# Attention and mixture of experts on one core: a constant tile 96 bytes longer, six staging tiles for weights instead of four, and an offset for one block of the first expert

## The chip, the cores and the metric

The kernel runs on one core of one Trainium2 chip. The metric is the time of one execution on the device in microseconds (us); the median of several runs counts. The engines are named as in the profile: PE (matrix products), PEld (PE's loading of weights), DVE (VectorE), ACT (ScalarE), POOL (GpSimd) and SP (SyncE, which here issues transfers).

## What is computed

The reference has two halves. The first is attention for 2 batches of 8 heads, 768 tokens and 64 columns a head, where a token looks only at the tokens with its own hash bucket. The second sends each of the 1,536 rows of 512 columns that come out to one of 8 experts:

```python
h = np.maximum(x[b, s] @ w1[e], 0.0)
out[b, s] = p[e] * (h @ w2[e])
```

Here `w1[e]` is 512 x 1024 and `w2[e]` is 1024 x 512, in float32. Routing is top 1, and a row may keep the expert of the row before it.

## The kernel before

The attention half comes first. An order written out by hand (`ORDER`) sets what each engine does there. It ends at about 251 us with the rows of the first expert gathered and transposed. From then on the experts follow one another, 256 slots each, and a scheduler of the language orders the instructions on each engine.

An expert has two layers. **The hidden layer** (`hidden`, L688) has four blocks of 24 matmuls with 256 moving columns each. Every float32 operand is split into a high and a low part (`wh` and `wl`, `xH` and `xL`, `hH` and `hL`), and three of the four products are summed. The weights of `w1` are the stationary operand (`lhsT`), the rows of x the moving one. After each block ACT writes `hH` (L690) and DVE writes `hL` (L691). **The output layer** (`expert`, L798) has for each half of the slots (t = 0 and 1) 24 matmuls with 512 moving columns. Here `hH` and `hL` are stationary and the parts of `w2` move. The last expert cuts its second half into two pieces of 256 columns. Between the two layers of an expert, eight transposes (`xprep`, L765) turn the rows of the next expert. Expert 0 differs: its weights and rows come through tiles left from the attention half.

**Weights** (`weights`, L750) come in pieces of 512 KB, four of `w1` and four of `w2` an expert. SP issues the transfer into a staging tile `st` of the pool `wst` (L752), ACT makes `wh` (L754), DVE makes `wl` (L755). The staging tile is free again after L755. The parts of `w1` have room for one expert (`w1p`, 8 tiles), those of `w2` for two (`w2p`, 16 tiles). The rows of expert e+1 (`xsl`, L761) come through the same queue of SP into one of two tiles. That tile is free when the scatter of expert e-1 to the output has landed (`out`, L808, issued by POOL).

**Addresses.** Pools are laid out from both ends of a partition's memory. From the left, in this order, stand among others the constants with `OV` in their middle, `w2p`, `hp` (`hH`, `hL`) and `mp` (`xsl`, `xH`, `xL`). From the right stand `wst`, then `w1p`. The tiles are placed by the program, not by chance, and the addresses that follow are those of the built program. `XOFF` (40 words) shifts `xH` and `xL` inside their tiles, and `HOFF` shifts the last of the four blocks of `hH` and `hL` of the experts that it names, by words of 4 bytes:

```python
HOFF = {1: 62, 2: 62, 3: 32, 4: 16, 5: 62, 6: 16}
hH, hL = (wide(hp, [128, 2, 256], n, HOFF.get(e, 0) if i == 3 else 0, 64) for n in ("hH", "hL"))
xH, xL = (wide(mp, [128, 4, 256], n, XOFF, 64) for n in ("xH", "xL"))
```

By distance this text means the address at which the running matmul begins to read its moving operand, less the address from which the next matmul's weights are loaded, modulo 256 bytes.

Of the kernel before, what the change touches and what calls it, by code (L numbers as in the profile page):

```python
# [6 lines left out]
F32 = mybir.dt.float32  # L7
# [9 lines left out]
CAP = 256  # L17
NE = 8
XOFF = 40
HOFF = {1: 62, 2: 62, 3: 32, 4: 16, 5: 62, 6: 16}  # L20

# [95 lines left out]
def tile_kernel(ctx, tc, qT, kT, v, proj, wg, w1, w2, cst, out):  # L119
    nc = tc.nc  # L120
    const = ctx.enter_context(tc.tile_pool(name="const", bufs=1))
# [30 lines left out]

    xs = dram.tile([NE * CAP, 514], F32, name="xs")
    xo = dram.tile([5 * CAP, 514], F32, name="xo")
    OV = const.tile([1, 16], F32, name="OV")
    ni = const.tile([1, 1], I32, name="ni")
    be = const.tile([1, 5], I32, name="be")
    EC = [const.tile([128, 2, 6, 8], F32, name=f"ec{b}") for b in range(2)]
# [242 lines left out]
    def fill_some(k):  # L401
        for _ in range(min(k, len(fills))):
            o, i = fills.pop()
            nc.sync.dma_start(out=o, in_=i)

    def fill(dst, z, zi):
        n = dst.shape[0] // 128
        nc.gpsimd.memset(z, 0.0)
        nc.gpsimd.iota(zi, pattern=[[128, n]], base=2048, channel_multiplier=1)
        xv = dst.rearrange("(t p) c -> p t c", p=128)  # L410
        fills.extend((xv[:, o:o + m, 0:513], z[:, 0:513].unsqueeze(1).to_broadcast([128, m, 513])) for o in range(0, n, 2) for m in (2,))
        with nc.allow_non_contiguous_dma(reason="one word per row"):
            nc.sync.dma_start(out=xv[:, :, 513].bitcast(I32), in_=zi)
# [103 lines left out]
    def overflow_count():  # L517
        row = [const.tile([1, 8], F32, name=f"cr{i}") for i in range(2)]
        nb = const.tile([1, 8, 5], F32, name="nb")
        nc.sync.dma_start(out=row[0], in_=CU[1])  # L520
        nc.vector.tensor_tensor(out=row[1], in0=row[0], in1=cs[0:1, 144:152], op=ALU.subtract)
        nc.vector.scalar_tensor_tensor(out=nb, in0=row[1].unsqueeze(2).to_broadcast([1, 8, 5]), scalar=1.0 / CAP,
                                       in1=cs[0:1, 188:193].unsqueeze(1).to_broadcast([1, 8, 5]), op0=ALU.mult, op1=ALU.is_gt)
        nc.vector.tensor_reduce(out=row[1], in_=nb, axis=AX.X, op=ALU.add)
        nc.vector.tensor_tensor_scan(out=OV[:, 8:16], data0=row[1], data1=row[1], initial=0.0, op0=ALU.add, op1=ALU.max)
        nc.vector.tensor_tensor(out=OV[:, 0:8], in0=OV[:, 8:16], in1=row[1], op=ALU.subtract)
        nc.vector.tensor_copy(out=ni, in_=OV[:, 15:16])
        bt = const.tile([1, 5, 8], F32, name="bt5")
        bf = const.tile([1, 5], F32, name="bf5")
        nc.vector.tensor_tensor(out=bt, in0=OV[:, 8:16].unsqueeze(1).to_broadcast([1, 5, 8]),  # L530
                                in1=cs[0:1, 188:193].unsqueeze(2).to_broadcast([1, 5, 8]), op=ALU.is_le)
        nc.vector.tensor_reduce(out=bf, in_=bt, axis=AX.X, op=ALU.add)
        nc.vector.tensor_copy(out=be, in_=bf)
# [136 lines left out]
    def wide(pool, shape, name, o, pad):  # L670
        n = shape[1] * shape[2]
        return pool.tile([128, n + pad], F32R, tag=name, name=name)[:, o:o + n].rearrange("p (a b) -> p a b", a=shape[1])

    def hidden(e, W1, X1, between=None):
        hs = []
        for i in range(4):
# [9 lines left out]
            for k, n in order:  # L686
                w, x = terms[k][n]
                nc.tensor.matmul(out=hps[:, k], lhsT=w, rhs=x, start=(k, n) in ends[0], stop=(k, n) in ends[1])  # L688
            hH, hL = (wide(hp, [128, 2, 256], n, HOFF.get(e, 0) if i == 3 else 0, 64) for n in ("hH", "hL"))
            nc.scalar.activation(out=hH, in_=hps, func=ACTF.Relu)  # L690
# [52 lines left out]
        hs0 = hidden(0, first_w, lambda c: [x[:, c % 2] for x in X0[c // 2]], second)  # L743
    rctx.close()
    mp = ctx.enter_context(tc.tile_pool(name="mp", bufs=2, reuse_waits="tile"))
    wst = ctx.enter_context(tc.tile_pool(name="wst", bufs=4, reuse_waits="tile", side="right"))
    w1p = ctx.enter_context(tc.tile_pool(name="w1p", bufs=8, reuse_waits="tile", side="right"))
    OC = []

# [8 lines left out]
    def xprep(slots, queue=nc.sync, after=None):  # L758
        xsl = mp.tile([128, 2, 514], F32, tag="xsl", name="xsl")
        with tc.issue_after(after) if after else nullcontext():  # L760
            queue.dma_start(out=xsl, in_=slots.rearrange("(t p) c -> p t c", p=128))  # L761
        xps = pvp.tile([128, 4, 256], F32, tag="pv", name="xps")
        for c in range(4):
            for t in range(2):
                nc.tensor.transpose(xps[:, c, 128 * t:128 * t + 128], xsl[:, t, 128 * c:128 * c + 128], idf)  # L765
        xH, xL = (wide(mp, [128, 4, 256], n, XOFF, 64) for n in ("xH", "xL"))
        LAST["x"] = (nc.scalar.activation(out=xH, in_=xps, func=ACTF.Copy).ins,
                     nc.vector.tensor_tensor(out=xL, in0=xps, in1=xH.bitcast(F32), op=ALU.subtract).ins)
        return xsl[:, :, 512:514], xH, xL
# [47 lines left out]
    for e in range(NE):  # L817
        xt = expert(e, w1[e], w2[e], xt, (lambda: xprep(xs[CAP * (e + 1):CAP * (e + 2)], nc.sync if e else nc.gpsimd, LAST["SP"] if e else None)) if e + 1 < NE else None,
                    None if e else hs0)
        if e == 0:  # L820
            with tc.issue_after(LAST["DVE"]):
                overflow_count()
        if e == 2:
            n_ovf = nc.values_load(ni[0:1, 0:1], min_val=0, max_val=5, skip_runtime_bounds_check_because="1536 tokens in blocks of 256")

    with tc.If(n_ovf > 0):
        z = mp.tile([128, 514], F32, tag="xsl", name="zo")
        zi = const.tile([128, 10], I32, name="zio")
        fill(xo, z, zi)
        fill_some(5)  # L830
        o1 = const.tile([1, 128], F32, name="o1")
        nc.vector.memset(o1, 1.0)
        ovp = py.tile([128, 512], F32, tag="yps", name="ovp")
        nc.tensor.matmul(out=ovp[:, 0:8], lhsT=o1, rhs=OV[:, 0:8])
        ova = const.tile([128, 8], F32, name="ova")
        nc.vector.tensor_copy(out=ova, in_=ovp[:, 0:8])
        v1 = const.tile([128, 6, 8], F32, name="v1")
        v2 = const.tile([128, 6, 8], F32, name="v2")
        v3 = const.tile([128, 6], F32, name="v3")
        for b in range(2):  # L840
            V_ = nc.vector
            bc = [128, 6, 8]
            lim = cs[:, 144:152].unsqueeze(1).to_broadcast(bc)
            V_.tensor_tensor(out=v1, in0=EC[b][:, 1], in1=lim, op=ALU.is_le)
            V_.scalar_tensor_tensor(out=v1, in0=v1, scalar=16384.0, in1=EC[b][:, 1], op0=ALU.mult, op1=ALU.add)
            V_.tensor_tensor(out=v1, in0=v1, in1=lim, op=ALU.subtract)
            V_.tensor_scalar(out=v2, in0=ova.unsqueeze(1).to_broadcast(bc), scalar1=float(CAP),
                             scalar2=-1.0, op0=ALU.mult, op1=ALU.add)
            V_.tensor_tensor(out=v1, in0=v1, in1=v2, op=ALU.add)
            V_.tensor_tensor(out=v1, in0=v1, in1=EC[b][:, 0], op=ALU.mult)  # L850
            V_.tensor_reduce(out=v3, in_=v1, axis=AX.X, op=ALU.add)
            so = const.tile([128, 6], I32, name=f"so{b}")
            V_.tensor_copy(out=so, in_=v3)
            for q in range(6):
                nc.gpsimd.indirect_dma_start(
                    out=xo[:, :], out_offset=bass.IndirectOffsetOnAxis(ap=so[:, q:q + 1], axis=0),
                    in_=XT[b][:, q], in_offset=None, bounds_check=5 * CAP - 1, oob_is_err=False)
        with tc.For_i(0, n_ovf, 1) as it:
            OC.clear()
            ev = nc.values_load(be[0:1, bass.ds(it, 1)], engines=(mybir.EngineType.SP,), min_val=0, max_val=NE - 1,  # L860
                                skip_runtime_bounds_check_because="expert of a block that exists")
            expert(0, w1[bass.ds(ev, 1)].rearrange("a d f -> (a d) f"), w2[bass.ds(ev, 1)].rearrange("a f d -> (a f) d"),
                   xprep(xo[bass.ds(it * CAP, CAP)]))
# [34 lines left out]
```

## Time and profile before

| | before |
|---|---|
| median of 3 runs | 447.32 us (447.24 to 448.72) |
| the profiled execution, its own time | 447.12 us |
| its span, first to last instruction | 445.2 us |
| PE busy | 431.6 us, 97% |
| granted TensorE clock, mean | 0.996 of full speed |

Times in the views are microseconds from the start of the span. The profiled execution is 1.9 us longer than its span and 0.20 us shorter than the median. A matmul's row gives its start and its length; matmuls overlap, so what one costs is the step from its start to that of the next.

### The profile page before, as it was taken

To read this page: it belongs to the slowest core of one execution; us is meant where nothing else is said; L and a number is where in the kernel's file an instruction comes from. 1 tells how busy PE (TensorE), PEld (TensorE's weight loads), DVE (VectorE), ACT (ScalarE), POOL (GpSimd) and SP (SyncE) were. 2 spreads that over 40 slices of the span, in tenths; PEclk is the share of its full clock that TensorE was granted. 3 is DMA by queue.
4 is the path that set the end of the run, shared out by engine and by line. 5 is a ranking of instruction groups with operands and counts; after the bars stand their busy time and mean duration, and the time that the engine had idled before them with its cause. 6 is when DMAs were issued, how large, how long until landed. Compare 5 with 4: busy or idle time off the path is not lost.

```text
span 445.2 us, 8348 instructions
## 1 busy us (share of the span) xinstructions
PE 431.6 (97%) x3320; PEld 339.8 (76%) x3320; DVE 286.5 (64%) x454; ACT 206.8 (46%) x284; POOL 169.7 (38%) x121
## 2 busy tenths in 40 slices
PE   8989999999999999999999999999999999999993
PEld 6976585747567567766665999989798989898993
DVE  5866777768557677686988856765656564738110
ACT  2045273626526355362744347664555555546110
POOL 5228946537888646959153122020101000000001
PEclk9999999999999999999999999999999999999998
DMA  5621241205163100310252169988758586854000
GB/s 184 176 84 41 69 145 42 71 15 163 55 201 116 37 13 6 109 35 3 96 190 107 46 240 315 314 280 273 242 190 280 176 240 224 254 166 142 37 1 32
DMA packets 42633, 60.20 MB, mean 135 GB/s; under 512 B 5469, under 2 KB 25149, under 8 KB 42592
## 3 DMA queue, kind: packets, MB, share of 16 engines
q1 hardware_dynamic: 38972, 50.36, 35.8%
q0 software_dynamic: 2432, 6.84, 4.0%
q10 hardware_dynamic: 1188, 2.45, 1.8%
q8 instruction: 27, 0.44, 0.4%
q14 instruction: 14, 0.11, 0.1%
HBM read 47.69 MB, written 11.56 MB: 133 GB/s over the span
## 4 chain that ended last, share of the span: by engine, by line
PE 77%; issue 10%; DMA 5%; DVE 5%; POOL 1%; ACT 1%; SPq 0%; POOLq 0%; DVEq 0%
PE s L214 24%; PE pv L278 15%; PE hps L688 13%; PE yps L798 11%; DMA st<-w 3%; PE busy L565 3%; PE ug L372 3%; PE hb L182 1%; POOL out L808 1%; PE st L330 1%; PE xt L665 1%; DVE wl L755 1%; DMA hw<-proj 1%; PE pv L285 1%; PE xps L765 1%
## 5 line engine op out<-in xcount | busy, mean ns | idle before, releaser
L223 DVE TENSOR_REDUCE mx<-s 128x2 f32<-128x768 f32 x96 | 88.8, 952 | 34.5 <-PE s L214 33.9
L755 DVE TENSOR_TENSOR wl<-st,wh 128x1024 fp32r<-128x1024 f32 x56 | 67.8, 1220 | 56.1 <-ACT wh L754 55.8
L264 ACT ACTIVATE pt<-s 128x768 f32<-128x768 f32 x96 | 74.2, 811 | 45.9 <-PE s L214 44.3
L271 POOL TENSOR_TENSOR sp<-sp,pt 128x768 f32<-128x768 f32 x40 | 75.1, 1889 | 39.5 <-DVE sp L271 29.9
L754 ACT ACTIVATE wh<-st 128x1024 fp32r<-128x1024 f32 x56 | 59.1, 1058 | 42.8 <-DMA st<-w 22.1
L214 PE MATMUL s<-hx 64*128 64x384 f32 x384 | 71.7, 368 | 0.8 <-DVE mx L223 0.8
L278 PE MATMUL pv<-pt,v 128*64 128x384 f32 x384 | 69.7, 495 | 0.0
L808 POOL DMA_INDIRECT out<-y,xsl x13 | 13.4, 1028 | 143.5 <-ACT y L801 134.6
L214 PE MATMUL s<-b,b 64*128 64x384 f32 x384 | 65.3, 334 | 0.0
L688 PE MATMUL hps<-xH,wh 128*128 128x256 f32 x224 | 56.2, 284 | 0.0
L688 PE MATMUL hps<-xH,wl 128*128 128x256 f32 x224 | 56.0, 280 | 0.0
L214 PEld LDWEIGHTS s<-hx 64*128 64x128 f32 x384 | 36.2, 183 | 23.6 <-ACT pt L264 6.9
L798 PE MATMUL yps<-wh,hH 128*128 128x512 f32 (+1 forms) x136 | 52.2, 384 | 0.0
L798 PE MATMUL yps<-wh,hL 128*128 128x512 f32 (+1 forms) x136 | 51.7, 380 | 0.2 <-DVE hL L691 0.2
L798 PE MATMUL yps<-wl,hH 128*128 128x512 f32 (+1 forms) x136 | 51.4, 378 | 0.0
L278 PEld LDWEIGHTS pv<-pt,v 128*64 128x64 f32 x384 | 24.5, 136 | 31.7 <-issue 30.9
L688 PEld LDWEIGHTS hps<-xH,wl 128*128 128x128 f32 x224 | 42.3, 189 | 0.3
L688 PEld LDWEIGHTS hps<-xH,wh 128*128 128x128 f32 x224 | 42.0, 188 | 0.3
L214 PEld LDWEIGHTS s<-b,b 64*128 64x128 f32 x384 | 36.6, 185 | 0.0
L688 PE MATMUL hps<-xL,wh 128*128 128x256 f32 x224 | 35.9, 282 | 0.0
L214 PE MATMUL s<-hx,lx 64*128 64x384 f32 x192 | 32.7, 334 | 0.0
L214 PE MATMUL s<-lx,hx 64*128 64x384 f32 x192 | 32.6, 333 | 0.0
(196 smaller groups left out, 630.8 us busy)
## 6 DMA issues: line engine op xcount, KB each, us to landing
st<-w SPq DMA_DIRECT2D x56, 512.0 KB
xs<-z SPq DMA_DIRECT2D x8, 513.0 KB
st<-w SPq DMA_DIRECT2D x13, 256.0 KB
xsl<-xs SPq DMA_DIRECT2D x6, 514.0 KB
v<-v SPq DMA_DIRECT2D x12, 256.0 KB
xq<-qT SPq DMA_DIRECT2D x6, 384.0 KB
xk<-kT SPq DMA_DIRECT2D x5, 384.0 KB
xk<-kT ACTq DMA_DIRECT2D x3, 384.0 KB
```

The costliest lines, as they stand in the source:

```text
L214: nc.tensor.matmul(out=sc[:, h, 0:384], lhsT=w[r, cols[0]], rhs=x[r, cols[1]], tile_position=(64 * h, 0), start=first and n == 0, stop=las ...
L223: nc.vector.tensor_reduce(out=MX[p][:, kh, i // 3, :, i % 3], in_=sc[:, :, 0:384], axis=AX.X, op=ALU.max)
L264: nc.scalar.activation(out=pt.rearrange("p (a q) -> p a q", a=2), in_=sc[:, :, 0:384], func=ACTF.Exp, scale=0.125)
L271: eng.tensor_tensor(out=SP[p, h], in0=PT[p, 0, h] if kt == 1 else SP[p, h], in1=PT[p, kt, h], op=ALU.add)
L278: nc.tensor.matmul(out=PV[p][64 * h:64 * h + 64, half, 0:384], lhsT=V[b, kt][:, pp * 128 + 64 * h:pp * 128 + 64 * h + 64], rhs=PT[p, kt, h ...
L372: nc.tensor.matmul(out=t[:, half, j * 146:j * 146 + 146], lhsT=OT[p][:, q * 128:q * 128 + 128], rhs=iw[:, pp])
L565: nc.tensor.matmul(out=IDLE[0][:, i, 0:384], lhsT=Fl[64 * i:64 * i + 64, 0:128], rhs=Fl[64 * i:64 * i + 64, 0:384], tile_position=(64 * i, 0))
L688: nc.tensor.matmul(out=hps[:, k], lhsT=w, rhs=x, start=(k, n) in ends[0], stop=(k, n) in ends[1])
L754: nc.scalar.activation(out=H, in_=st, func=ACTF.Copy)
L755: nc.vector.tensor_tensor(out=L, in0=st, in1=H.bitcast(F32), op=ALU.subtract)
L798: nc.tensor.matmul(out=yps[:, us], lhsT=h[:, k, ts], rhs=w[:, k, us], start=(n == 0), stop=(n == 23))
L808: i = nc.gpsimd.indirect_dma_start(out=dst, out_offset=bass.IndirectOffsetOnAxis(ap=idx, axis=0), in_=y[:, us], in_offset=None, bounds_che ...
```

## The change

There are four edits. `OV` takes 40 words and uses the first 16, so that everything placed after it from the left moves by 96 bytes. `HOFF` gains an entry for expert 0. `wst` gets six tiles. The load of the count `ni`, on which the branch at the end depends, is written after the loop over the experts and not inside it.

```diff
-HOFF = {1: 62, 2: 62, 3: 32, 4: 16, 5: 62, 6: 16}
+HOFF = {0: 62, 1: 62, 2: 62, 3: 32, 4: 16, 5: 62, 6: 16}
...
-    OV = const.tile([1, 16], F32, name="OV")
+    OV = const.tile([1, 40], F32, name="OV")[:, 0:16]
...
-    wst = ctx.enter_context(tc.tile_pool(name="wst", bufs=4, reuse_waits="tile", side="right"))
+    wst = ctx.enter_context(tc.tile_pool(name="wst", bufs=6, reuse_waits="tile", side="right"))
...
-        if e == 2:
-            n_ovf = nc.values_load(ni[0:1, 0:1], min_val=0, max_val=5, skip_runtime_bounds_check_because="1536 tokens in blocks of 256")
-
+
+    n_ovf = nc.values_load(ni[0:1, 0:1], min_val=0, max_val=5, skip_runtime_bounds_check_because="1536 tokens in blocks of 256")
```

In the built program these distances result:

| matmuls | before | after |
|---|---|---|
| hidden layer, expert 0 | 192 | 192 |
| hidden layer, experts 1 to 7 | 96 | 192 (64 short of 256) |
| output layer, blocks without offset | 0 | 0 |
| output layer, last block of expert 0 | 0 | 8 |
| attention, `pv` (L278) | 128 | 224 |

For experts 1 to 7 a moving operand of expert 1 stood at 154176 and a weight tile at 180192, 26016 apart downward, which is 96 modulo 256. Now they stand at 154272 and 172000. Expert 0's stand at 201120 and 192480, 8640 apart, which is 192.

The scheduler reorders the transfers and the copies of weights. On SP's queue, this is the piece from the weights of expert 2 on. `128x4x256` is a piece of `w1`, `128x2x512` one of `w2`, `xsl` the rows of the expert after. The first unmarked pair is `w2` of expert 2 and `w1` of expert 3, and the first `xsl` is that of expert 3:

```order
 L752 DMA st<-w 128x2x512 x4
 L752 DMA st<-w 128x4x256 x4
+L752 DMA st<-w 128x2x512 x2
 L761 DMA xsl<-xs 128x2x514
+L752 DMA st<-w 128x2x512 x2
+L752 DMA st<-w 128x4x256 x4
 L752 DMA st<-w 128x2x512 x4
+L761 DMA xsl<-xs 128x2x514
```

The rows of expert 3 now stand behind two pieces of `w2` of expert 3, which they preceded. From expert 4 on `xsl` stands behind all eight pieces of its expert and not between `w1` and `w2`.

On ACT this is the stretch of expert 2, from the copy after the output of expert 1 (`y`) to the copies of the rows of expert 3 (`xH`). Before:

```order
L801 ACTIVATE y<-yps,xsl 128x512
L754 ACTIVATE wh<-st 128x1024
L690 ACTIVATE hH<-hps 128x512
L754 ACTIVATE wh<-st 128x1024
L690 ACTIVATE hH<-hps 128x512
L754 ACTIVATE wh<-st 128x1024
L690 ACTIVATE hH<-hps 128x512
L754 ACTIVATE wh<-st 128x1024 x2
L690 ACTIVATE hH<-hps 128x512
L754 ACTIVATE wh<-st 128x1024
L767 ACTIVATE xH<-xps 128x1024
```

And of the change, the same stretch:

```order
L801 ACTIVATE y<-yps,xsl 128x512 x2
L754 ACTIVATE wh<-st 128x1024 x2
L690 ACTIVATE hH<-hps 128x512
L754 ACTIVATE wh<-st 128x1024 x2
L690 ACTIVATE hH<-hps 128x512
L754 ACTIVATE wh<-st 128x1024
L690 ACTIVATE hH<-hps 128x512
L754 ACTIVATE wh<-st 128x1024 x2
L690 ACTIVATE hH<-hps 128x512
L754 ACTIVATE wh<-st 128x1024
L767 ACTIVATE xH<-xps 128x1024
```

In both, two pieces of `w2` of expert 3 are copied just ahead of the last `hH` of expert 2. Before they were the first two pieces, now they are the third and fourth, and the first two are copied earlier. The instructions of DVE follow the same order. PE's order does not change, and the load of `ni` stands last on each engine in both programs.

## Rows read from the trace of the kernel before

**Rows 1.** The page's first part: busy us, share, instructions

```profile
PE 431.6 (97%) x3320; PEld 339.8 (76%) x3320; DVE 286.5 (64%) x454; ACT 206.8 (46%) x284; POOL 169.7 (38%) x121
```

**Rows 2.** Chain that ended last, from 239 us: start, length, what

```profile
251.09 11.04 PE hps L688 x96
...
273.96 11.52 PE hps L688 x96
...
305.55 6.04 DMA st<-w
...
321.31 11.52 PE hps L688 x96
...
344.72 11.51 PE hps L688 x96
```

**Rows 3.** Timeline of PE, third block of expert 0's hidden layer

```profile
256.52 0.62 PE L688 MATMUL hps<-x0H,b 128*128 128x256 f32 x4
...
259.24 0.62 PE L688 MATMUL hps<-x0H,w 128*128 128x256 f32 x4
```

**Rows 4.** Timeline of PE, third block of expert 2's hidden layer

```profile
302.99 0.28 PE L688 MATMUL hps<-xH,wh 128*128 128x256 f32 x1
...
305.87 0.28 PE L688 MATMUL hps<-xH,wh 128*128 128x256 f32 x1
```

**Rows 5.** Timeline of PE, last expert, output in pieces of 256 columns

```profile
434.08 0.28 PE L798 MATMUL yps<-wl,hH 128*128 128x256 f32 x1
...
436.96 0.28 PE L798 MATMUL yps<-wl,hH 128*128 128x256 f32 x1
```

**Rows 6.** Timeline of PE around the one wait of expert 2

```profile
308.75 1.04 PE L765 MATMUL xps<-cs,xsl 128*128 128x128 f32 x8
...
314.00 0.40 PE L798 MATMUL yps<-wl,hH 128*128 128x512 f32 x1
...
314.94 0.40 PE L798 MATMUL yps<-wh,hH 128*128 128x512 f32 x1
```

**Rows 7.** Timeline of ACT there; in brackets idle time, releaser

```profile
311.62 1.06 ACT L754 ACTIVATE wh<-st 128x1024 fp32r<-128x1024 f32 x1 [0.78 <-DMA st<-w]
312.59 0.58 ACT L690 ACTIVATE hH<-hps 128x512 fp32r<-128x512 f32 x1
```

**Rows 8.** Timeline of DVE there

```profile
313.86 0.69 DVE L691 SCALAR_TENSOR_TENSOR hL<-hps,hH 128x512 fp32r<-128x512 f32 x1
```

**Rows 9.** Timeline of SP: weights of expert 1, rows of experts 3, 4

```profile
262.15 2.80 SPq L752 DMA_DIRECT2D st<-w  x4
...
304.58 0.37 SPq L761 DMA_DIRECT2D xsl<-xs  x1
...
325.52 0.37 SPq L761 DMA_DIRECT2D xsl<-xs  x1
```

**Rows 10.** Timeline of POOL: last scatters of experts 1 and 2

```profile
298.45 0.97 POOL L808 DMA_INDIRECT out<-y,xsl  x1 [2.72 <-ACT y L801]
...
322.36 0.97 POOL L808 DMA_INDIRECT out<-y,xsl  x1 [3.57 <-ACT y L801]
```

**Rows 11.** Waits of SP's queue: us in total, times, longest

```profile
SPq L761 <- DMA out<-y,xsl: 33.9, 5, 7.8
```

**Rows 12.** Busy time by stretch, last columns PE clock, DMA share, GB/s

```profile
268.70:283.00 14.30, 14.30 (x105) 13.46 (x104) 10.44 (x10) 10.59 (x13) 2.60 (x2) 1.00 0.97 312
```

**Rows 13.** Timeline of PE: a last block at distance 0 (expert 0)

```profile
265.62 0.39 PE L798 MATMUL yps<-wl,hH 128*128 128x512 f32 x1
...
266.97 0.39 PE L798 MATMUL yps<-wl,hH 128*128 128x512 f32 x1
```

**Rows 14.** Timeline of PE: a last block at distance 8 (expert 1)

```profile
290.10 0.40 PE L798 MATMUL yps<-wh,hL 128*128 128x512 f32 x1
...
291.50 0.39 PE L798 MATMUL yps<-wh,hL 128*128 128x512 f32 x1
```

**Rows 15.** The page's fifth part: `pv`; busy us, mean ns of one

```profile
L278 PE MATMUL pv<-pt,v 128*64 128x384 f32 x384 | 69.7, 495 | 0.0
```

## The prediction

> **What bounds the kernel now.** I read the page's first part first: PE is busy 97% of the span, DVE 64% and ACT 46% [rows 1]. The chain of waits then says which PE work counts. From 251 us on it is hardly anything but PE: 96 matmuls of a hidden layer, eight transposes, 48 matmuls of an output layer, expert after expert, with one detour over a transfer at 305.55 [rows 2]. So whatever shortens a matmul in this stretch shortens the kernel, and whatever only brings weights earlier does not, except at that detour.
>
> The reader should compare the hidden layers in the chain. Experts 1, 3 and 4 take 11.52, 11.52 and 11.51 us, expert 0 takes 11.04, although all have the same 96 matmuls of the same shape [rows 2]. The timeline shows it free of stops. In expert 0 the third block begins at 256.52 and the fourth at 259.24: 24 matmuls in 2.72 us, 113.3 ns each [rows 3]. In expert 2 the same block takes from 302.99 to 305.87: 2.88 us, 120.0 ns each [rows 4]. No wait stands in these rows. What differs is the distance in the table above: 192 in expert 0, 96 in the others. The last expert's pieces of 256 columns, at distance 0, also take 120.0 ns (24 matmuls from 434.08 to 436.96) [rows 5]. So 120 is not a property of the hidden layer, and of the three distances at which 256 columns move, 192 alone runs at 113.3.
>
> **The change part by part.** *Longer `OV`.* It brings experts 1 to 7 to the distance of expert 0. If the distance sets the rate, each block gains 2.88 - 2.72 = 0.16 us [rows 3, 4], and seven experts with four blocks gain 28 x 0.16 = 4.48 us. The bounds are nothing (the distance is not the cause) and 4.48. I take 4.48: the rows stand nearest to this case, and with either of the two `xH` tiles the distance after the change is that of expert 0 modulo 256.
>
> The SBUF page of the Trainium skill (SBUF — State Buffer, section "Who interferes with whom") speaks against this term. It gives PE two separate read ports, one for the moving operand and one for loading weights, and says that PE and ACT wait for no one. By it the term would be nothing. The trace differs, with 113.3 against 120.0 ns.
>
> The same edit moves the operands of other matmuls. In `pv` the distance goes from 128 to 224. That is 384 records of 495 ns, 69.7 us [rows 15], of two passes and two concurrent halves, so 192 steps. No row shows `pv` at 224. If each step gained or lost what a hidden matmul does between the two distances, 6.7 ns, it would be 1.3 us either way. I take nothing, since such a plain float32 product is none of those that showed a difference, and keep both ends for the range. The distances inside the score products and in the output layer stay as they are. DVE and ACT read at other distances too, but they have the slack of [rows 1].
>
> *The offset in expert 0.* With distance 0 the last block of expert 0 takes 1.35 us for six matmuls (265.62 to 266.97) [rows 13]. Expert 1's, at distance 8, takes 1.40 (290.10 to 291.50) [rows 14]. Two passes over the block cost 0.10 us. It could also set how expert 1's hidden layer, which follows, enters. No row shows that, as every hidden layer after an offset runs at distance 96 today. The bounds are a loss of 0.10 and, if expert 1 would otherwise stay slow, its whole 0.64. As the 4.48 already counts expert 1 as fast, I take a cost of 0.10.
>
> *Six staging tiles.* The only stop of PE that a transfer causes is in expert 2. From 314.00 to 314.94 two steps take 0.94 us, where 0.23 each is usual (1.40 us for six) [rows 6, 14]. The excess is 0.48. PE waits there for `hL` of the last block, which DVE starts at 313.86 [rows 8]. Its `hH` ran at 312.59 on ACT, behind a copy of weights that began at 311.62 after 0.78 us of waiting for its transfer [rows 7]. That transfer was issued behind the rows of expert 3 (304.58) [rows 9], and these had waited for the scatter of expert 1, which started at 298.45 [rows 10]. SP's queue waits like this in five places, 33.9 us in all [rows 11].
>
> After the change the same two copies still stand ahead of that `hH`, and the transfers that they need are still issued behind `xsl`. So the question is when `xsl` goes out. Let hL follow the issue of `xsl` as today, by 314.55 (end of `hL`) - 304.58 = 9.97 us. PE wants it at 314.00 + 0.23, less the gain of two hidden layers, of which the offset takes some back (1.28 - 0.10 = 1.18), so at 313.05. `xsl` must go by 303.08. The scatter of expert 1 starts 0.54 earlier, at 297.9. Today it takes 6.13 us from there to `xsl` (298.45 to 304.58), with weight transfers in the way. The one of expert 2, with fewer in the way, takes 3.16 (322.36 to 325.52) [rows 9, 10]. With 3.16 `xsl` goes at 301.1 and nothing stops; with 6.13 it goes at 304.0 and PE stops 0.97 us. The early stretch moves 312 GB/s [rows 12]. Ahead of `xsl` are 22 pieces of 512 KB and two sets of rows, 12.6 MB: 40 us at that rate. Today the first four go out at 262.15, when expert 0's hidden layer has freed their place [rows 9]. With six tiles the first piece takes a place that was freed before that layer began, and two more can be under way. A queue that flows from about 258 on is empty at about 298, when the scatter starts. I take the short time: the 0.48 goes.
>
> *The load of `ni`* stands last on each engine before and after. It costs nothing, and there is no cover that could be lost.
>
> The sum is made against the profiled execution's own 447.12 us: 447.12 - 4.48 - 0.48 + 0.10 = 442.26. That execution lies 0.20 below the median, so the forecast is 442.5.
>
> **Rivals.**
> (a) *`hL` of expert 2 is still late.* The scatter lands as slowly as today, PE stops 0.97 us: 443.4. If `xsl` went no earlier than today, PE would wait to 314.6 whatever it gained before, and only experts 3 to 7 would count: 447.32 - 5 x 0.64 = 444.1. For it speak the two pieces newly ahead of `xsl`, against it the earlier start.
> (b) *Some hidden layers stay slow.* The distance is right but the state in which the output layer leaves PE keeps a layer at 120 ns. In expert 0 nothing of that kind is seen: its third block is even. Each such layer gives back 0.64; one to four make 443.1 to 445.1.
> (c) *The distance is without effect.* Something else makes expert 0 fast, such as where its tiles lie. Then only 0.48 - 0.10 is gained: 446.9. Against it stands that distance 0 and 96 give the same 120.0 in different layers and tiles. This is the time that the SBUF page's rule gives.
> (d) *Slower: the rows come too late.* From expert 4 on `xsl` stands behind `w2` of its expert, and PE needs the rows right after the hidden layer before. Today the chain from the start of that layer is 1.05 us to the scatter (321.31 to 322.36), 3.16 to `xsl`, and at most 4.17 until the transposes (304.58 to 308.75): 8.4 us [rows 2, 6, 9, 10]. The layer will last 10.88, so 2.5 us are free. With the scatter at 6.13 it would be 11.35, 0.47 late in each of five experts: 444.9. It decides the sign when each comes 1.4 us late (3.9 us more than in the short chain): 442.5 + 5 x 1.4 = 449.5.
>
> **How the numbers follow.** The forecast (442.2 to 442.9, or with `pv` 1.3 us either way, 441.2 to 443.8) has a chance of 0.69. (a) has 0.13, (b) 0.07, (c) 0.06, (d) 0.05, of which 0.03 ends slower. I call a change that this measurement can tell half a per cent, 2.2 us. Below 445.08 lie the forecast, (a), nearly all of (b) and a part of (d): 0.89. Within the bound lie (c) and the rest: 0.08. Slower is 0.03. The range takes in the forecast with half of what `pv` could gain, (a) and (b): 441.6 to 445.1. It leaves out (c), the slow end of (d) and the edge of `pv`, together about 0.13.
>
> **What will show it.** Right: every hidden layer from expert 1 on is a row of 96 matmuls at about 10.9 us in the chain, a block steps 2.72 us, and the third expert's output layer has no step above 0.24 but its first. Expert 0's last block takes 1.40 us in place of 1.35. `xsl` of expert 3 goes out before 303. `pv` stays at 69.7 us. Wrong: layers at 11.5 (c, or b if only some), a wait of PE for `hL` (a), a wait of the transposes for `xsl` (d), or a different length of the attention half.

## The result, and the profile after

The changed kernel takes **442.44 us** (median of 4 runs, 442.40 to 443.08) against 447.31 for the kernel before on the same chip (4 runs, 447.24 to 448.72): a ratio of 0.9887, 95% interval [0.9866, 0.9908]. The forecast was 442.5. The profiled execution took 442.4 us with a span of 440.6, where the one of before had 447.12 and 445.2.

On the page of the changed kernel (busy us, share, instructions; then the group of `pv`) PE is still the engine that fills the span, and busy time and mean length of `pv` are what they were [rows 1, 15]:

```profile
PE 427.4 (97%) x3320; PEld 335.9 (76%) x3320; DVE 286.1 (65%) x454; ACT 207.3 (47%) x284; POOL 169.1 (38%) x121
...
L278 PE MATMUL pv<-pt,v 128*64 128x384 f32 x384 | 69.7, 495 | 0.0
```

Lengths alone would not show a change of rate: a matmul of the hidden layers is recorded with about 0.28 us whether the next one starts 113.3 or 120.0 ns after it. But `pv` steps as it did, too. A row of eight records, first to last, takes 1.51 us at distance 128 (before) and at 224 (changed):

```profile
33.78 1.51 PE L278 MATMUL pv<-pt,v 128*64 128x384 f32 x8
...
33.79 1.51 PE L278 MATMUL pv<-pt,v 128*64 128x384 f32 x8
```

The timeline of the changed kernel through expert 2 (start, length, engine, line, what) holds most of the answer:

```profile
297.92 0.97 POOL L808 DMA_INDIRECT out<-y,xsl  x1 [4.03 <-ACT y L801]
...
300.36 0.62 PE L688 MATMUL hps<-xL,wh 128*128 128x256 f32 x4
...
300.86 0.37 SPq L761 DMA_DIRECT2D xsl<-xs  x1
...
303.08 0.62 PE L688 MATMUL hps<-xL,wh 128*128 128x256 f32 x4
...
310.10 0.69 DVE L691 SCALAR_TENSOR_TENSOR hL<-hps,hH 128x512 fp32r<-128x512 f32 x1
...
313.07 0.40 PE L798 MATMUL yps<-wh,hL 128*128 128x512 f32 x1
```

A row of four equal matmuls stands in every group of twelve, so two rows of one kind, 24 matmuls apart, are one block: 300.36 to 303.08, 2.72 us or 113.3 ns a matmul, where the block of [rows 4] took 2.88. `xsl` goes out at 300.86, not 304.58 [rows 9]; the last `hL` is done at 310.79, and PE takes it at 313.07 without a stop. Before, `hL` was done at 314.55 [rows 8], and PE sat idle until it took it at 314.60 (timeline of before, idle time and releaser in brackets):

```profile
314.60 0.50 PE L798 MATMUL yps<-wh,hL 128*128 128x512 f32 x1 [0.20 <-DVE hL L691]
```

The same timeline at the last block of expert 0, now at an offset: 1.40 us to the next pass, 1.35 before [rows 13].

```profile
266.08 0.39 PE L798 MATMUL yps<-wh,hH 128*128 128x512 f32 x1
...
267.48 0.40 PE L798 MATMUL yps<-wh,hH 128*128 128x512 f32 x1
```

The chain of waits has to be read with care here. In the changed kernel it does not run along PE any more:

```profile
251.09 11.06 PE hps L688 x96
...
276.74 15.78 issue
292.75 1.14 POOL out L808
293.89 3.80 issue
```

It follows POOL's own queue, and "issue" stands where the profile shows nothing that POOL waits for. POOL does not bound the kernel; the stretches between its scatters are PE's layers. So the layers have to be read from the timeline, not from the chain as in [rows 2].

Windows over a hidden layer of expert 0 and one of expert 1 with its transposes (busy time by engine, then PE's clock, DMA share, GB/s) show a granted clock of 1.00 of full speed in both, the higher of its two levels (2.4 GHz). [rows 12] shows the same for a stretch of the kernel before that holds most of a layer at 120.0 ns, so these two rates are no matter of the clock:

```profile
251.09:262.00 10.91, 10.91 (x97) 10.91 (x98) 8.39 (x16) 6.89 (x12) 3.54 (x3) 1.00 0.69 214
273.90:285.60 11.70, 11.70 (x106) 11.70 (x104) 10.90 (x12) 9.56 (x13) 1.67 (x1) 1.00 1.07 367
```

### The profile page after: what moved, and what is told of

It reads as the page before. It is cut to its first block, busy times and chain, and to the rows that moved or that the text cites. A ratio compares the mean times of both kernels' runs of the same rounds, so it can differ in the third digit from the quotient of the medians.

```text
span 440.6 us, 8349 instructions
## 1 busy us (share of the span) xinstructions
PE 427.4 (97%) x3320; PEld 335.9 (76%) x3320; DVE 286.1 (65%) x454; ACT 207.3 (47%) x284; POOL 169.1 (38%) x121
## 4 chain that ended last, share of the span: by engine, by line
PE 54%; issue 35%; POOL 4%; DVE 4%; DMA 1%; ACT 1%; POOLq 0%; SPq 0%; DVEq 0%
PE s L214 24%; PE pv L278 14%; PE busy L565 4%; POOL out L808 4%; PE ug L372 3%; PE hps L688 3%; PE hb L182 1%; PE st L330 1%; PE xt L665 1%; PE pv L285 1%; DVE sp L271 1%; PE st L339 1%; PE vt L543 0%; DVE mx L223 0%; DMA Fl<-nt 0%
## 5 line engine op out<-in xcount | busy, mean ns | idle before, releaser
L278 PE MATMUL pv<-pt,v 128*64 128x384 f32 x384 | 69.7, 495 | 0.0
L754 ACT ACTIVATE wh<-st 128x1024 fp32r<-128x1024 f32 x56 | 58.0, 1057 | 23.6 <-DMA st<-w 11.5
L688 PE MATMUL hps<-xH,wh 128*128 128x256 f32 x224 | 53.8, 276 | 0.0
L688 PE MATMUL hps<-xH,wl 128*128 128x256 f32 x224 | 53.7, 277 | 0.0
L278 PEld LDWEIGHTS pv<-pt,v 128*64 128x64 f32 x384 | 24.4, 136 | 31.7 <-issue 30.9
L691 DVE SCALAR_TENSOR_TENSOR hL<-hps,hH 128x512 fp32r<-128x512 f32 x32 | 21.9, 685 | 20.0 <-ACT hH L690 19.2
L688 PE MATMUL hps<-xL,wh 128*128 128x256 f32 x224 | 34.5, 276 | 0.0
```

Of the source, the lines that this page charges most:

```text
L278: nc.tensor.matmul(out=PV[p][64 * h:64 * h + 64, half, 0:384], lhsT=V[b, kt][:, pp * 128 + 64 * h:pp * 128 + 64 * h + 64], rhs=PT[p, kt, h ...
L691: LAST["DVE"] = nc.vector.scalar_tensor_tensor(out=hL, in0=hps, scalar=0.0, in1=hH.bitcast(F32), op0=ALU.max, op1=ALU.subtract).ins
L754: nc.scalar.activation(out=H, in_=st, func=ACTF.Copy)
```

## The experiments

The table gives, for each profiled execution, the ns of one matmul in the hidden layers of experts 0 to 7 (66 matmuls from the middle of the layer, by their starts), and the time for which PE stopped in experts 2 and 3 for a transfer (layer against the same layer without a stop). The profiled execution need not be the median one: for offset_16 and distance_112 it is the slowest of its runs. Medians stand as measured; the kernel before took 446.8 to 447.5 beside them. Of experts 1 to 7 the distance is 96 where a layer shows 120.0, 112 in distance_112, and 192 in the others; of expert 0 it is always 192.

| kernel | median us | e0 | e1 | e2 | e3 | e4 | e5 | e6 | e7 | stops us |
|---|---|---|---|---|---|---|---|---|---|---|
| before | 447.3 | 113.3 | 120.0 | 120.0 | 120.0 | 120.0 | 120.0 | 120.0 | 120.0 | 0.48 |
| changed | 442.44 | 113.3 | 113.3 | 113.3 | 113.3 | 113.3 | 113.3 | 113.3 | 113.3 | 0 |
| after_again | 442.78 | 113.3 | 113.3 | 113.3 | 113.3 | 113.3 | 113.3 | 113.3 | 113.3 | 0 |
| distance_back | 446.95 | 117.8 | 120.0 | 120.0 | 120.0 | 120.0 | 120.0 | 120.0 | 120.0 | 0 |
| distance_alone | 444.67 | 113.3 | 117.8 | 117.8 | 117.8 | 117.8 | 113.3 | 117.8 | 113.3 | 0 |
| six_staging_alone | 446.69 | 113.3 | 120.0 | 120.0 | 120.0 | 120.0 | 120.0 | 120.0 | 120.0 | 0 |
| four_staging | 444.87 | 113.3 | 113.3 | 113.3 | 113.3 | 113.3 | 113.3 | 113.3 | 113.3 | 2.3 |
| no_offset_0 | 443.22 | 117.8 | 117.8 | 113.3 | 113.3 | 113.3 | 113.3 | 113.3 | 113.3 | 0.2 |
| no_offsets | 445.03 | 117.8 | 117.8 | 117.8 | 117.8 | 117.8 | 117.8 | 117.8 | 117.8 | 0 |
| offset_16 | 444.18 | 117.8 | 113.3 | 113.3 | 113.3 | 113.3 | 113.3 | 113.3 | 113.3 | 2.0 |
| half_offset | 442.46 | 113.3 | 117.8 | 113.3 | 113.3 | 113.3 | 113.3 | 113.3 | 113.3 | 0 |
| distance_112 | 442.72 | 117.8 | 113.3 | 113.3 | 113.3 | 113.3 | 113.3 | 113.3 | 113.3 | 0.7 |

**Is it the distance?** `distance_back` undoes it alone:

```diff
-XOFF = 40
+XOFF = 16
```

> The changed kernel in all its parts, but with XOFF = 16 instead of 40, so that the hidden layers of experts 1 to 7 stand at distance 96 again, while the longer OV, the six staging tiles and the offset in expert 0 stay. Theory (the distance alone sets the rate): these layers go back from 2.72 to 2.88 us a block and from about 10.91 to 11.52 us each, 7 x 0.61 = 4.3 us, so 442.4 + 4.3 = 446.7 us; the stop in expert 2 stays away. Rival (what counts is where the longer OV and the wider staging put the tiles, not this distance): blocks stay at 2.72 us and the time at 442.4.

It took 446.95 us (10 runs, 446.47 to 448.07), ratio to before 0.9988 [0.9972, 1.0004]. Its timeline in expert 2 has the block of [rows 4] again:

```profile
301.79 0.64 PE L688 MATMUL hps<-xL,wh 128*128 128x256 f32 x4
...
304.67 0.64 PE L688 MATMUL hps<-xL,wh 128*128 128x256 f32 x4
```

2.88 us: tiles, pools and staging as in the changed kernel, only the rows of x 96 bytes lower inside their tiles, and nearly the whole gain is gone. (In this profile 0.41 us of it is expert 0, which took 117.8 and which the edit does not touch.) The rival of the tiles' place falls. `distance_alone` goes the other way, from the kernel before:

```diff
-XOFF = 40
+XOFF = 64
```

> The kernel before with XOFF = 64 instead of 40 and nothing else: the hidden layers of experts 1 to 7 stand at distance 192, with OV short, four staging tiles and no offset in expert 0. Theory (the distance alone sets the rate, and the staging tiles alone remove the stop in expert 2): hidden layers at about 10.91 us, blocks at 2.72, 4.3 us gained; the stop in expert 2 stays at 0.48 us if the rows of expert 3 go out earlier by what PE gains, 443.1, and grows to 1.70 us if they go out when they did (304.6), 444.3. So 443.1 to 444.3. Rival 1 (the tiles' place): 447.3. Rival 2 (the stop goes by itself when the scatter of expert 1 comes earlier, and the staging tiles do nothing): 442.6.

444.67 us (4 runs, 444.44 to 445.21), ratio 0.9949 [0.9929, 0.9969]. The time lies above the expected interval, and for another reason than a stop. The timeline shows expert 2, then expert 5:

```profile
301.05 0.64 PE L688 MATMUL hps<-xL,wh 128*128 128x256 f32 x4
...
303.88 0.63 PE L688 MATMUL hps<-xL,wh 128*128 128x256 f32 x4
...
370.48 0.62 PE L688 MATMUL hps<-xL,wh 128*128 128x256 f32 x4
...
373.20 0.62 PE L688 MATMUL hps<-xL,wh 128*128 128x256 f32 x4
```

Same shape, same distance, no wait, and 2.83 against 2.72 us: **at 192 there are two steady rates**, 117.8 and 113.3 ns, and in these profiles a layer keeps to its end the one that it has settled on. Neither theory had this. Five of the seven layers took the longer one, 0.40 us each. The stop of expert 2 was absent, so rival 2 was right there. The granted clock was 1.00 in a layer at the longer rate as well (expert 1, same columns as above):

```profile
274.10:285.30 11.20, 11.20 (x97) 11.20 (x96) 8.84 (x10) 7.86 (x10) 1.38 (x1) 1.00 0.95 327
```

**What chooses between the two rates?** `no_offset_0` takes the new offset away:

```diff
-HOFF = {0: 62, 1: 62, 2: 62, 3: 32, 4: 16, 5: 62, 6: 16}
+HOFF = {1: 62, 2: 62, 3: 32, 4: 16, 5: 62, 6: 16}
```

> The changed kernel without HOFF[0]. Theory (the offset is only a cost): the last block of expert 0 takes 1.35 us again in each of its two passes, 0.08 us less, 442.36 us, and the hidden layer of expert 1 runs as it does with it (2.75 us for the first block, 2.72 after). Rival (the offset sets how the next layer enters): expert 1 stays at 120 ns a matmul, 11.5 us, and the time is 0.6 us longer, 442.97.

443.22 us (4 runs, 442.82 to 443.71), ratio 0.9911 [0.989, 0.9932]. The timeline, expert 1 and then expert 2:

```profile
278.08 0.63 PE L688 MATMUL hps<-xL,wh 128*128 128x256 f32 x4
...
280.91 0.64 PE L688 MATMUL hps<-xL,wh 128*128 128x256 f32 x4
...
301.19 0.62 PE L688 MATMUL hps<-xL,wh 128*128 128x256 f32 x4
...
303.91 0.62 PE L688 MATMUL hps<-xL,wh 128*128 128x256 f32 x4
```

Expert 1, entered without an offset, steps 2.83; expert 2, entered after one, 2.72. The rival was right in kind: the offset sets how the next layer runs, though the rate it avoids is 117.8 and not 120. The rest of the distance from 442.44 to this profile's 443.53 is mostly expert 0's own layer at 117.8 (0.41 us) and a wait of 0.2 us in expert 3. `no_offsets` drops all of them, and `offset_16` asks whether the pattern of distance_alone (short after an offset of 16, long after 62, 32 or none) was the offset's doing; it is distance_alone with

```diff
-HOFF = {1: 62, 2: 62, 3: 32, 4: 16, 5: 62, 6: 16}
+HOFF = {0: 16, 1: 16, 2: 16, 3: 16, 4: 16, 5: 16, 6: 16}
```

> The changed kernel without any offset (HOFF empty). Theory (a layer that is entered from an output layer without offset takes the slow steady rate, as expert 1 did in no_offset_0): experts 1 to 7 at 117.8 ns, 7 x 0.40 = 2.8 us more, and some 0.09 us less in each of seven output layers, 0.6: 442.44 + 2.8 - 0.6 = 444.6 us. Rival 1 (expert 1 was slow in no_offset_0 because expert 0 had been slow there, and without offsets a layer keeps the rate of the one before): all layers alike, 441.8 in runs in which expert 0 is fast and 444.6 and 0.4 more in the others. Rival 2 (the offsets are only a cost): 441.8.

> The kernel before with XOFF = 64 (hidden layers of experts 1 to 7 at distance 192, as in distance_alone) and with an offset of 16 in the last block of each of the experts 0 to 6. In distance_alone the layers that were entered after an offset of 16 (experts 5 and 7) ran at 113.3 ns a matmul, those after an offset of 62 or 32 or after none at 117.8, 0.40 us a layer more. Theory (at 192 there are two steady rates, and the offset ahead of a layer decides which one it takes): all seven layers at 113.3, 444.67 - 5 x 0.40 + 0.08 for the new offset in expert 0 = 442.75 us. Rival (the tiles' place or chance decides, not the offset): experts 1 to 4 and 6 stay at 117.8, or others do, and the time is near 444.7.

no_offsets: 445.03 us (4 runs, 444.63 to 445.39), ratio 0.9949 [0.9933, 0.9966], all seven layers at 117.8, as the first theory had it. Expert 0 was at 117.8 in this profile too, so by itself it does not exclude that layers hand the rate on; distance_alone does for its own layout, with expert 0 at 113.3 and expert 1, entered without an offset, at 117.8, and half_offset below shows the same pair in the layout of the changed kernel. offset_16: 444.18 us (4 runs, 444.01 to 445.09), ratio 0.9926 [0.991, 0.9943], 1.4 above the theory; but all seven layers are at 113.3, as it said. What it had left out is PE's stop in expert 2, 2.0 us in the profiled run of 445.09 (timeline, idle time and releaser in brackets):

```profile
309.62 1.06 PE L765 MATMUL xps<-cs,xsl 128*128 128x128 f32 x8 [1.02 <-DMA xsl<-xs]
...
315.75 0.50 PE L798 MATMUL yps<-wh,hL 128*128 128x512 f32 x1 [0.50 <-DVE hL L691]
```

With four staging tiles and short layers, both the transposes for expert 3 and the last `hL` come late.

**What are the staging tiles worth?** `four_staging` is the changed kernel with `bufs=4` for `wst`, `six_staging_alone` the kernel before with `bufs=6`.

> The changed kernel with four staging tiles. Theory (six tiles are what removes the stop in expert 2): the stop is back, with 0.48 us if everything moves along and 1.70 if the rows of expert 3 go out no earlier than before (304.6), 442.9 to 444.1 us. Rival (the stop hung on a few tenths of a us in the queue of transfers, and goes when PE's times move at all, as in distance_alone): 442.4, with the rows of expert 3 going out at about 304 and the last hL of expert 2 a few tenths before PE wants it.

> The kernel before with six staging tiles and nothing else: distance 96 in experts 1 to 7. Theory: hidden layers stay at 11.52 us, blocks at 2.88; the stop in expert 2 goes, 447.46 - 0.48 = 446.98 us. Rival (the gain of the change comes from the staging tiles and their place): near 442.4. Rival (the tiles do nothing): 447.46 with a stop of 0.48 us.

four_staging: 444.87 us (5 runs, 443.42 to 445.86), ratio 0.994 [0.9916, 0.9964]. The rows of expert 3 go out at 305.31, and PE stops at the same two places as in offset_16:

```profile
309.39 1.06 PE L765 MATMUL xps<-cs,xsl 128*128 128x128 f32 x8 [1.49 <-DMA xsl<-xs]
...
315.39 0.50 PE L798 MATMUL yps<-wh,hL 128*128 128x512 f32 x1 [0.33 <-DVE hL L691]
```

Against the changed kernel the layer and its transposes are 1.67 us longer and the output layer 0.65: 2.3 us, more than the 1.70 taken as the worst case. six_staging_alone: 446.69 us (10 runs, 446.24 to 447.5), ratio 0.9983 [0.9973, 0.9993], `xsl` out at 301.75, no stop, layers at 120.0, as its theory said. So the tiles are worth half a us at distance 96 (0.48 in the profiles, 0.8 between the medians) and over two at 192.

four_staging says one thing more. Its layers are all at 113.3 after the same offsets of 62 and 32 that left them at 117.8 in distance_alone, so the staging tiles are not what makes those offsets work. Of what else differs for experts 2 to 7 the longer `OV` and the place of the load of `ni` remain, beside the `XOFF` that gives both kernels the same distance; no run takes either of them alone.

**How does the rate hang on the distance?** Two kernels give each of the experts 1 to 7 its own `XOFF` (56, 0, 8, 24, 32, 48, 40, and 36, 38, 42, 44, 52, 60, 20).

> The changed kernel with another XOFF for each expert: 56, 0, 8, 24, 32, 48, 40 for experts 1 to 7, which puts their hidden layers at the distances 0, 32, 64, 128, 160, 224 and 192 bytes modulo 256. Theory (the rate is a function of the distance): 120.0 ns for a matmul at 0, as in the last expert's pieces, 113.3 at 192, and for the others some value from 113.3 to 120.0 that is the same in all four blocks of the layer after its entry; the whole between 442.4 and 442.4 + 6 x 0.61 = 446.1 us. Rival (a state that a layer keeps from the one before, or the tiles' place): all layers at 113.3 and 442.4, or rates that change within a layer.

> The changed kernel with XOFF = 36, 38, 42, 44, 52, 60, 20 for experts 1 to 7: distances 176, 184, 200, 208, 240, 16 and 112 bytes modulo 256. Theory (the rate is a smooth function of the distance, with its least value near 192): 184 and 200 below 115 ns, 176 and 208 between those and the 117.5 and 117.9 seen at 160 and 224, 240 and 16 between 116.7 and 120.0, 112 between 118.8 and 120.0; some 444.5 us. Rival (113.3 is one of two steady patterns at one exact distance): no layer at 113.3 but expert 0, all between 116.7 and 120.0, 442.44 + 7 x 0.4 to 0.64 = 445.2 to 446.9 us.

They took 445.71 and 446.13 us, one run each. Worked out from the starts of 60 or 72 matmuls in the timeline:

| distance | 0 | 16 | 32 | 64 | 96 | 112 | 128 | 160 | 176 | 184 | 192 | 200 | 208 | 224 | 240 |
|---|---|---|---|---|---|---|---|---|---|---|---|---|---|---|---|
| ns | 120.0 | 116.7 | 116.7 | 117.8 | 120.0 | 113.3 | 118.7 | 117.3 | 119.3 | 120.0 | 113.3 or 117.8 | 120.5 | 119.2 | 118.3 | 117.1 |

The rate is no smooth function: 8 bytes to either side of 192 cost all of the gain. Both expectations missed something, the theory this sharpness, the rival the 113.3 at 112. Except for 96 and 192, each is here one layer with one entry, so another entry could give another rate.

Is it the distance, or the moving operand's own address? The hidden layers do not part the two, as their weights begin at 224 modulo 256 in all these kernels (180192, 172000 and 192480 do). The last expert's pieces of 256 columns help. `OV` moved their two operands together by 96 bytes, and they take 120.0 ns before and in the changed kernel. In `half_offset` below only their weights move, to distance 192, and 24 of them take 2.83 us, 117.8 ns each (its timeline):

```profile
428.04 0.28 PE L808 MATMUL yps<-wh,hH 128*128 128x256 f32 x1
...
430.87 0.28 PE L808 MATMUL yps<-wh,hH 128*128 128x256 f32 x1
```

Both speak for the distance. No run moves the weights of a hidden layer alone, so for the whole table it is not shown.

For 112 another entry was tried, in all layers and without offsets:

```diff
-XOFF = 40
+XOFF = 20
-HOFF = {0: 62, 1: 62, 2: 62, 3: 32, 4: 16, 5: 62, 6: 16}
+HOFF = {}
```

> The changed kernel with XOFF = 20 and no offsets: hidden layers of experts 1 to 7 at distance 112, the second distance at which a layer ran at 113.3 ns (expert 7 of map_fine, entered after an offset of 16). Theory 1 (at 112 there are two rates as at 192, and a layer entered from an output layer without offset takes the slow one): all seven layers well above 113.3 ns, 117.8 if the slow rate is the same, and about 445.0 us as in no_offsets. Theory 2 (at 112 there is only the fast rate): all seven at 113.3 without any offset, the output layers 0.09 us shorter each, 442.44 - 0.6 = 441.8 us, less than the changed kernel takes.

442.72 us (6 runs, 441.91 to 443.58), ratio 0.9899 [0.9884, 0.9914]. The timeline of expert 1:

```profile
275.63 0.63 PE L688 MATMUL hps<-xL,wh 128*128 128x256 f32 x4
277.01 0.61 PE L688 MATMUL hps<-xL,wh 128*128 128x256 f32 x4
278.37 0.61 PE L688 MATMUL hps<-xL,wh 128*128 128x256 f32 x4
```

The first interval of twelve matmuls is 1.38, the next 1.36: without an offset all seven layers fall into 113.3 within their first block. So theory 2 was right on the rate, yet the median is that of the changed kernel and not 441.8. In this profile, of the slowest run (443.58), expert 0 took the longer rate (0.41 us), and the rows of expert 4 came late, 0.74 us from the layer to the transposes:

```profile
331.84 1.07 PE L765 MATMUL xps<-cs,xsl 128*128 128x128 f32 x8 [0.55 <-DMA xsl<-xs]
```

**Could less of an offset do?** `half_offset`, its core (the tile of expert 7 has a gap of 16 elements between its halves in each block):

```diff
-hH, hL = (wide(hp, [128, 2, 256], n, HOFF.get(e, 0) if i == 3 else 0, 64) for n in ("hH", "hL"))
+o = 32 if i == 3 else 0
+hH, hL = (hp.tile([128, 576], F32R, tag=n, name=n)[:, 0:512 + 2 * o].rearrange("p (k x) -> p k x", k=2)[:, :, 0:256] for n in ("hH", "hL"))
```

> The changed kernel with two edits that the runs so far point to. Experts 0 to 6: in the last inner block only the second half of the hidden rows (k = 1) is shifted, by 32, so three of its six matmuls stand at distance 128 and three at 0. Expert 7: each hidden block leaves 16 elements between its two halves of rows, so that the pieces of 256 columns stand at distance 192 and the 512-column pass stays at 0 (its two results a block are written by two instructions each on ACT and DVE). Theory (a few shifted matmuls right ahead of a layer are enough to send it into the fast rate): experts 1 to 7 at 113.3 ns, output layers 0.04 us shorter each, 0.3 in all, and 47 pieces of 256 columns 6.7 ns shorter each, 0.32, or 0.10 if they take the 117.8 of the slow steady rate: 441.8 to 442.1 us. Rival (the whole block has to be shifted): up to seven layers at 117.8, 0.40 us each, up to 444.6.

> The changed kernel once more, for the spread and beside half_offset. Theory: experts 1 to 7 at 113.3 ns again (each is entered after an offset), expert 0 at 113.3 or at 117.8 (it is entered without one, after a wait, and took either in the runs so far, 0.41 us apart): 442.4 or 442.9 us. Rival (chance decides in each layer): some of experts 1 to 7 at 117.8 as well, and times up to 445.2.

half_offset: 442.46 us (5 runs, 442.11 to 443.74), ratio 0.9903 [0.9885, 0.992]; the changed kernel beside it 442.78 (4 runs, 442.07 to 443.18), 0.99 [0.9883, 0.9918], all its layers at 113.3 as its theory had it. The median lies above the 441.8 to 442.1 expected, the profiled run (442.11) at its upper end. Three shifted matmuls are enough for six of seven layers, not for expert 1, which runs at 117.8 although expert 0 ran at 113.3. The pieces of 256 columns went from 120 to 117.8 ns, the longer rate of 192 again. No version here beats the changed kernel by more than a measurement can tell.

## Why the prediction held, step by step

**The first term.** It said 4.48 us for 28 blocks. By the starts in the two timelines, the seven layers with what follows until the output layer are 0.57 to 0.61 us shorter each, 4.16 together. The part that is missing is the entry: the first block of each layer takes 2.75 us, not 2.72, five matmuls of 116 to 124 ns before the steady 113.3. That the place of the moving operand is the cause is shown by distance_back, where undoing those 96 bytes alone brings back 120.0 in all seven layers. Beyond the three distances that the prediction knew, 112 runs at 113.3 too, and 192 itself can run at 117.8. The rule of the SBUF page of the Trainium skill weighed there (section "Who interferes with whom") would have left the hidden layers of all these kernels alike; the runs differ, with 113.3 to 120.5 ns where only `XOFF` was changed. Whether the two reads of PE hold each other up or something else does it, no run shows.

**The offset.** This is the step that was wrong in sign. I priced it as 0.10 us of loss and let the first term count expert 1 as short anyway. The loss is there, 0.08 us over the two passes. But without the offset expert 1 runs at 117.8 (no_offset_0), 0.40 us more, so by these two profiles the edit is worth 0.32 and the first term rests on it and on the six offsets that were there already. Here the forecast was lucky: it gave those six no part, and without any offset (no_offsets) all seven layers run at 117.8 and the kernel takes 445.03 us. The mechanism was rival (b)'s, the state in which the output layer leaves PE, which got 0.07, with 0.64 a layer where the runs showed 0.40. Expert 0's even third block, held against it, said nothing: an even layer can be at either rate.

**The staging tiles.** The stop is gone, 11.60 us to 11.11 in expert 2's output layer, 0.49 for the 0.48 forecast, and `xsl` went at 300.86 where 301.1 was worked out. The scatter took 2.94 us from its start to `xsl`, the short time; in after_again it took 4.09 (298.30 to 302.39), and `xsl` was still early enough. Rival (a) is what the kernel would have been without the tiles: 444.87, beyond its 444.1, since the rows went out later than before and the transposes waited as well.

**The rest.** `pv` unchanged at 69.7 us and with the same step: 0, as taken. The load of `ni` cost nothing either: from the start of the last matmul to the end of the span are 7.79 us before and 7.78 in the changed kernel. -4.16 - 0.49 + 0.08, and -0.06 over small shifts of the other output layers, make -4.63; the spans differ by 4.6.

**Rival (d)** was nearer than its price said. The chain for expert 4's rows, in the timeline of the changed kernel:

```profile
320.73 0.97 POOL L808 DMA_INDIRECT out<-y,xsl  x1 [4.54 <-ACT y L801]
...
325.63 0.37 SPq L761 DMA_DIRECT2D xsl<-xs  x1
...
330.44 1.06 PE L765 MATMUL xps<-cs,xsl 128*128 128x128 f32 x8
```

From the layer's start (319.52) to the scatter are 1.21 us, from scatter to `xsl` 4.90 and not the 3.16 that I carried over, and from there to the transposes 4.81. Together that is the whole layer, 10.92 us, so the 2.5 us of room were used up. The eight transposes take 1.06 us, against 1.03 in after_again, so the rows came only just in time, and that nothing was lost was luck. In no_offset_0 PE lost 0.2 us at this place and in distance_112 0.74.

**Open:** why the operands' places set the rate, and why an output layer's last matmuls decide which of two rates the next layer takes; the runs show both only as behaviour. One address that no run varies by itself is the one at the seam: in the built programs the last moving operand of an output layer stands 128 modulo 256 from the first weights of the next layer in distance_alone, and 224 in the changed kernel, as `OV` moved `w2p`. This may be why offsets of 62 and 32 do nothing in the one and work in the other.

## What to carry to other kernels

Where PE is the bound and equal matmuls step differently without a wait, compare the addresses of the moving operand and of the next weights modulo 256; here 96 bytes were worth 1% of the time. Test such an edit together with what precedes the loop, since a stretch can lock into either of two rates: distance_alone had the right distance and kept about half of the gain (5 x 0.2 + 2 x 0.6 of 4.2 us). When PE gets faster, look for the transfer that was just in time: the staging tiles were worth 0.5 us before and 2.3 after.

## What was not expected of the hardware

- At one distance (192) a run of equal matmuls has two steady rates, 113.3 and 117.8 ns, each held to the end of the layer. Which one is taken follows the entry: after a block shifted as a whole by 62, 32 or 16 always 113.3 in the changed kernel's layout, after 16 only in distance_alone's.
- Expert 0, entered from the last matmuls of the attention half, took 113.3 in eight of the fourteen profiled executions and 117.8 in six, 0.41 us apart, also where the code up to there was the same. Part of the spread between runs of one kernel can come from that. Its second matmul started 0.220 to 0.224 us after the first in the eight, and 0.226, 0.227 or 0.199 us after it in the six: a few ns at the entry go with the rate, though no run shows that they set it.
- At distance 112 the layer finds 113.3 within its first block after an unshifted output layer, at 192 it does not.
